# Attention with routed experts: block counts by rounding, and a written order of all steps

## The chip, the cores and the metric

The kernel runs on one core of one Trainium2 chip. The metric is the device time of one execution in microseconds (us), taken as the median of several runs. A core has five engines with queues of their own: TensorE (PE in the profile; PEld is its loading of weights), VectorE (DVE), ScalarE (ACT), GpSimd (POOL) and SyncE (SP), which here only issues DMAs. Each engine takes its instructions strictly in the order in which the program put them, so an instruction that waits holds up all that stand behind it on its engine.

## The reference

Random-feature attention over 8 batches, 8 heads, 576 positions and a head dimension of 64 with 128 features is followed by a mixture of experts with one expert for each token (4608 tokens of 512 numbers, 8 experts with a hidden width of 1024):

```python
def phi(x):
    h = einsum('bhsd,md->bhsm', x, omega) - sum(x * x, axis=-1, keepdims=True) / 2
    return exp(h - max(h, axis=-1, keepdims=True)) / sqrt(m)
q_p, k_p = phi(q * scale), phi(k * scale)
kv, z = einsum('bhsm,bhsd->bhmd', k_p, v), sum(k_p, axis=2)
x = einsum('bhsm,bhmd->bhsd', q_p, kv) / (einsum('bhsm,bhm->bhs', q_p, z)[..., None] + 1e-6)
...
logits = x @ w_gate
e_idx = argmax(logits, axis=1)
for e in range(E):
    mask = e_idx == e
    ye = maximum(x[mask] @ w1[e], 0) @ w2[e]
    out[mask] = gate_w[mask, None] * eom[mask, e, None] * ye
```

`gate_w` is the softmax probability of the chosen expert, `eom` the sigmoid of `x @ w_output_gate`. Between the two parts x is laid out as one row for each token.

## The kernel before

**Units.** The attention is cut into 32 units: four super-chunks of two batches (1152 tokens, nine tiles of 128) times eight heads. Unit `u` loads its keys and queries twice, transposed (`ld.t`) and natural (`ld.n`), and its values (`ld.v`). Its steps: `pp` projects in three groups (L631); `mx` takes the smallest number of each row (L650); `sqa` and `sqr` sum the squares (L556 on ScalarE for unit 0 and from unit 8 on, `fold` at L576 to L580 on GpSimd for units 1 to 7; then L561 or L590 on VectorE); `nb` makes the bias of the exponential (L657, L661); `ex` is the exponential (L667); `eh` and `el` cut it into two f16 halves (L691 on ScalarE, L693 on GpSimd); `eT` turns the queries' features by a DMA (units 8 on; `tq`, `th` and `tl` do it on TensorE before). `kv` multiplies keys by values (L766), `kvh`/`kvs` halve the product (L784, L786), `kt`, `ke`, `kg`, `gh`, `gl` bring in the gates (L804 to L827), `pn` multiplies by the queries (L840), `xf` divides (L849 to L853), `xh` and `xl` cut the result into halves (L870, L874), `rows` stores them to DRAM.

**Routing.** After the eighth unit of each super-chunk j, VectorE works out what goes to which expert, in chains of small instructions on tables of 8 to 192 columns: `route`, `counts` (on TensorE: the running number of earlier tokens of the same expert, L1017 to L1027), `ranks`, `places`, `gates`, `weigh`, then for group g = j `table`, `assign`, `lists`, `controls`, `gi`, `advance`. A block has 128 tokens of one expert. Whole blocks are counted by turning a float into an integer, shifting it right by 7 and turning it back (L1049 to L1053, L1074 to L1079).

**Items.** A block is an item `n`, at most 49 of them, of which 38 run for these inputs (there are 38 gathers at L1572). `gx` gathers its rows on GpSimd (L1572), `xt` turns them by a DMA, `hA` and `hB` are the two halves of the first product (L1609), `relu` and `rest` cut the hidden values into halves on ScalarE and VectorE (L1616, L1620), `out` is the second product (L1640, or L1632 for an item with at most 64 tokens), `os` scales (L1693), `put` scatters the rows to the output on GpSimd (L1682). In the last group `hB` also holds the first half of the second product, so that only `out.n.1` follows. Where the expert changes, `bring` loads the new weights and `sw` cuts them into f16 halves; from item 25 on this goes by quarters, `swh` on ScalarE (L474) and `swl` on VectorE (L478). Whether it happens is known on the chip only: each engine loads a flag into a register (`flag`) and jumps. Items 38 and on stand behind such a jump.

**The order.** Every step is registered with `plan.add` (or `plan.chain`, one step for each instruction of a chain), with its engine, an estimated cost, a rank and what it follows. `Plan.order` (L287) then plays the program through with those costs: it takes, again and again, the step of lowest rank among those that could start soonest, ranks being moved by the table `SHIFT` (L76). `emit` (L1720) writes the instructions in the order that comes out, and that fixes each engine's queue. The PSUM banks are given out in the same way: the one that came free first.

Below, a step is named as in `kvs.25` (step, unit) or `out.25.1` (step, item, half); `mx`, `ex`, `eh`, `el` count keys and queries (`el.63` is the queries of unit 31) in turn, and `nb` counts units; a trailing `s` as in `table.0.2s` is a step inside a chain.

Of the kernel before, what the change touches and what calls it, by code (L numbers as in the profile page):

```python
# [72 lines left out]
UNIT_STEPS = tuple("hi lo sqa sqr pp tq th tl eT kv kvh kvs kt ke kg gh gl pn xf xh xl lga vh vl".split())  # L73
SLOT_STEPS = tuple("gx xt hA hB relu rest out os put sw swh swl bring".split())

SHIFT = {  # L76
    "advance": (-91.89, -199.63, -64.41,),
    "again": (0.0, 0.0, 0.0, 31.03,),
    "assign": (94.42, 64.4, 10.74, -5.41,),
    "bounded": (17.08, 13.53, 102.01, -16.15,),  # L80
    "bring": (-149.34, -144.98, -146.36, 16.69,),
    "const": (-12.6,),
    "controls": (-6.33, -38.05, -43.46, 95.17,),
    "counts": (-129.68, -194.11, 15.85, -107.74,),
    "eT": (0.4, 138.19, 61.6, 50.0,),
    "eh.k": (-0.7, -0.7, -4.51, 129.09,),
    "eh.q": (-0.7, -150.18, -1.08, 50.41,),
    "el.k": (1.4, 1.4, -54.14, -117.65,),
    "el.q": (1.4, -16.84, 91.6, -1.02,),
    "ex.k": (-31.78, 38.41, -6.63, -47.76,),  # L90
    "ex.q": (-20.34, 43.13, -3.54, 100.75,),
    "flag": (1.44,),
    "gate_exps": (61.95, 151.43, -245.24, -105.03,),
    "gates": (198.78, 115.38, 308.76, 145.18,),
    "gh": (-114.02, 44.58, -83.1, -4.31,),
    "gi": (-45.91, -100.94, 157.46, 201.04,),
    "gid": (0.0, 0.0, 0.0, -258.93,),
    "gl": (-220.24, -52.52, 14.91, 135.3,),
    "gx": (-233.8, 53.3, 108.33, -107.89,),
    "hA": (202.43, 203.85, 165.91, 123.74,),  # L100
    "hB": (102.44, 10.62, 75.55, -131.59,),
    "hi": (-1.4, -9.33, -61.41, 41.14,),
    "ke": (-119.21, 53.41, -58.62, -21.2,),
    "kg": (10.71, -73.95, -95.07, 122.55,),
    "kt": (-83.5, 22.25, -22.42, -41.82,),
    "kv": (-21.36, -31.1, -28.61, -26.36,),
    "kvh": (-48.28, -277.94, -84.66, -68.07,),
    "kvs": (11.17, -54.16, -170.98, -1.28,),
    "ld.n": (-18.72, -45.88, 99.01, 42.74,),
    "ld.t": (-18.62, -9.42, -106.08, 12.44,),  # L110
    "ld.v": (-15.0, -168.92, 67.12, 3.22,),
    "lga": (-126.07, -176.33, -150.87, 10.21,),
    "limits": (0.0, 0.0, 0.0, -74.63,),
    "lists": (234.87, 96.12, 15.36, 88.59,),
    "lo": (0.3, -72.57, 152.95, 119.66,),
    "mx": (7.85, 3.5, 87.64, 51.53,),
    "nb": (-8.03, 66.86, 56.7,),
    "os": (25.69, -10.82, 137.36, 17.68,),
    "out": (144.39, 45.75, 2.51, -0.53,),
    "pid": (149.39, 102.18, 69.01, -48.7,),  # L120
    "places": (42.24, -56.95, -75.3, -34.34,),
    "pn": (-121.01, -17.46, -25.99, 68.57,),
    "pp": (-23.92, 181.9, -27.84, 189.02,),
    "put": (-10.97, -0.64, -26.58, 80.94,),
    "ranks": (84.94, -45.33, -111.8, 137.76,),
    "relu": (109.14, -112.65, 102.51, 25.06,),
    "rest": (90.98, 95.59, 184.25, -102.14,),
    "route": (56.37, 197.97, -111.62, 78.22,),
    "rows": (50.29, 102.01, 155.46, -159.35,),
    "scales": (66.65, -76.99, -69.39, 128.92,),  # L130
    "sqa": (-182.65, 164.78, 45.98, 169.51,),
    "sqr": (-47.23, 74.7, 121.64, -85.06,),
    "sw": (109.96, 40.72, -32.62,),
# [96 lines left out]

# [1552 lines left out]
```

## Time and profile before

| | us |
|---|---|
| median of 3 runs | 660.61 (658.88 to 662.42) |
| the profiled execution | 663.06 |
| its span, first to last instruction | 661.2 |
| TensorE busy in the span | 598.8 |
| VectorE busy | 430.0 |
| ScalarE busy | 411.8 |
| GpSimd busy | 368.7 |
| mean granted clock of TensorE | 0.964 |

A line of the profile's groups gives source line, engine, operation, output and inputs, shape, count, busy time in us, mean ns of one, and the idle time of the engine just before, with what ended it. A line of the timeline begins with the start and the length in us; in brackets stands the idle time before it and what ended that. A "q" behind an engine (ACTq, DVEq) is that engine's sequencer: a register or a jump. The table of stretches has busy us and the number of instructions of PE, PEld, DVE, ACT and POOL, then the granted clock of TensorE, the DMA engines' share and GB/s.

### The profile page before, as it was taken

What the parts mean: (1) busy time and instruction counts of PE and PEld (TensorE: products, weight loads), DVE (VectorE), ACT (ScalarE), POOL (GpSimd) and SP (SyncE); (2) the same over time, 40 slices, a digit from 0 to 9 for tenths busy, and PEclk for the clock granted to TensorE, in tenths of its full rate; (3) what the DMA queues carried; (4) which work ended last, traced back from release to release, by engine and by line L of the source; (5) the groups of instructions that cost most, each with busy time, mean ns of one, the idle gap of its engine ahead of it and who ended that gap; (6) DMA issues with size and microseconds to landing.
All of it is one profiled execution on the core that took longest, in us unless ns stands there. A gap on an engine that the chain in (4) does not pass through costs nothing. (4 is left out here: it accounts for less than half of the span.)

```text
span 661.2 us, 21673 instructions
## 1 busy us (share of the span) xinstructions
PE 598.8 (91%) x8444; PEld 463.2 (70%) x8444; DVE 430.0 (65%) x1140; ACT 411.8 (62%) x968; POOL 368.7 (56%) x263
## 2 busy tenths in 40 slices
...
GB/s 301 364 264 205 243 221 222 233 258 233 236 294 257 217 225 210 221 194 295 292 183 211 121 181 156 129 111 260 169 145 205 216 70 177 229 84 70 239 142 8
DMA packets 147041, 133.75 MB, mean 202 GB/s; under 512 B 104398, under 2 KB 127568, under 8 KB 145616
## 3 DMA queue, kind: packets, MB, share of 16 engines
...
## 5 line engine op out<-in xcount | busy, mean ns | idle before, releaser
L1609 PE MATMUL ph<-xt,w1h 128*128 128x128 f16 (+1 forms) x2432 | 203.3, 217 | 2.2 <-PE po L1632 1.0
L1609 PE MATMUL ph<-xt,w1l 128*128 128x128 f16 (+1 forms) x1216 | 199.6, 217 | 0.0
L667 ACT ACTIVATE ef<-pp,nb 128x128 f32<-128x128 f32 x576 | 162.7, 389 | 54.8 <-DVE nb L661 46.6
L1609 PEld LDWEIGHTS <-w1h 128*128 128x128 f16 x2432 | 180.4, 98 | 9.8 <-issue 3.1
L1620 DVE SCALAR_TENSOR_TENSOR hl<-ph,hh 128x512 f16<-128x512 f32 (+1 forms) x76 | 50.6, 666 | 117.9 <-ACTq L1538 73.2
L693 POOL TENSOR_TENSOR es<-ef,es 128x1152 f16<-128x1152 f32 x44 | 105.1, 2399 | 34.1 <-ACT es L691 28.9
L650 DVE TENSOR_REDUCE pp<-pp 128x3 f32<-128x384 f32 x192 | 103.7, 558 | 22.2 <-PE pp L631 16.8
L1609 PEld LDWEIGHTS <-w1l 128*128 128x128 f16 x1216 | 118.0, 98 | 0.0
L1572 POOL DMA_INDIRECT gx<-rows,gi x38 | 39.2, 1033 | 134.8 <-ACTq L1538 67.0
L1640 PE MATMUL po<-w2l,hh 128*128 128x512 f16 x280 | 106.9, 382 | 3.3 <-DVE w2l L478 3.3
L1640 PE MATMUL po<-w2h,hl 128*128 128x512 f16 x280 | 106.8, 382 | 1.8 <-DVEq L1533 1.8
L1640 PE MATMUL po<-w2h,hh 128*128 128x512 f16 x280 | 107.0, 382 | 0.8 <-DVE hl L1620 0.8
L1640 PEld LDWEIGHTS <-hh 128*128 128x128 f16 x560 | 52.3, 99 | 57.0 <-issue 2.6
L1616 ACT ACTIVATE hh<-ph 128x512 f16<-128x512 f32 (+1 forms) x76 | 44.3, 584 | 69.8 <-PE ph L1609 63.8
L546 POOL TENSOR_TENSOR xlo<-xt,xhi 128x1152 f16<-128x1152 f32 x24 | 58.3, 2429 | 19.4 <-ACT xhi L539 19.2
L1693 ACT ACTIVATE os<-po,gx 128x512 f32<-128x512 f32 (+1 forms) x38 | 25.5, 672 | 69.1 <-PE po L1640 61.9
L840 PE MATMUL pn<-kvs,et 128*128 128x81 f16 (+1 forms) x960 | 47.9, 207 | 10.8 <-DVE kvs L827 4.3
L1640 PEld LDWEIGHTS <-hl 128*128 128x128 f16 x280 | 27.5, 98 | 39.6 <-issue 4.6
L840 PEld LDWEIGHTS <-et 128*128 128x128 f16 (+1 forms) x960 | 40.6, 103 | 19.1 <-issue 9.0
L691 ACT CAST es<-ef 128x1152 f16<-128x1152 f32 x44 | 50.8, 1173 | 2.7 <-DMA et<-es 2.7
L874 POOL TENSOR_TENSOR xs<-xf,xs 128x576 f16<-128x576 f32 x32 | 42.6, 1332 | 7.1 <-DVE xs L870 3.9
L631 PE MATMUL pp<-omh,xhi 64*128 64x128 f16 x432 | 42.8, 222 | 2.4 <-ACT ef L667 0.7
...
## 6 DMA issues: line engine op xcount, KB each, us to landing
...
```

Of the source, the lines that this page charges most:

```text
L546: lambda t0=t0, t1=t1: nc.gpsimd.tensor_tensor(out=xl(u)[:, t0:t1], in0=xt32(u)[:, t0:t1], in1=xh(u)[:, t0:t1], op=ALU.subtract),
L631: nc.tensor.matmul(banks["pp", 2 * u + i, g][:, c, :], x[r, t], w[r, :], start=(a == 0), stop=(a == len(ops) - 1))
L650: nc.vector.tensor_reduce(out=spare(g, 0)[:, i], in_=banks["pp", 2 * u + i, g][:, 0:3, :], op=ALU.min, axis=AX.X)
L667: nc.scalar.activation(ef(2 * u + i)[:, c, :], banks["pp", 2 * u + i, g][:, c % 3, :], AF.Exp, bias=nb(u)[:, i, c : c + 1], scale=-SK)
L691: nc.scalar.copy(es(slot_es(n))[:, 0], ef(n))
L693: nc.gpsimd.tensor_tensor(out=es(slot_es(n))[:, 1], in0=ef(n), in1=es(slot_es(n))[:, 0], op=ALU.subtract)
L840: nc.tensor.matmul(pn[lo:hi, c - c0, :], a[:, c, lo:hi], w[:, b, :], start=(i == 0), stop=(i == len(ops) - 1))
L874: nc.gpsimd.tensor_tensor(out=x[:, :, P + o : P + o + D], in0=xf(u)[:, :, 0:D], in1=x[:, :, o : o + D], op=ALU.subtract)
L1609: nc.tensor.matmul(ph[:, f4, 0:w_], w[qd][:, kk, fo : fo + P], xt(n)[:, x, 0:w_], start=(a == 0), stop=(a == 3 * KC - 1))
L1616: nc.scalar.activation(hh(n)[:, sl, 0:w_], banks["ph", n, g][:, :, 0:w_], AF.Relu)
L1620: nc.vector.scalar_tensor_tensor(out=hl(n)[:, sl, 0:w_], in0=banks["ph", n, g][:, :, 0:w_], scalar=0.0, in1=hh(n)[:, sl, 0:w_], op0=ALU.ma ...
L1640: nc.tensor.matmul(po, x(n)[:, f, :], w[f // 2][:, f % 2, :], start=(f == 0 and a == 0), stop=(f == FC - 1 and a == 2))
```

## The change

Three things are changed in the text of the kernel.

**Block counts by rounding.** All positions are kept as numbers of tokens, shifted by 63.5, and not as numbers of blocks. Adding and taking away 1.5 x 2^23 x 128, where a float has steps of 128, leaves the nearest multiple of 128: one instruction in place of three. The running count `cnt` goes into `counts` by two f32 matmuls with the identity, in place of an addition in `ranks`. `last` becomes the first column of `exs`, which saves a copy; the copy `cp` moves from `lists` to `places`.

```diff
+MIDDLE = (P - 1) / 2
+ROUND = 1.5 * 2.0**23 * P
...
 def counts(j):
-    nc.tensor.matmul(pos[:, 0:NC, :], tri, one, start=True, stop=False)
+    nc.tensor.matmul(pos[:, 0:NC, :], ident, cnt.unsqueeze(1).broadcast_to([P, NC, NE]), start=True, stop=False)
+    nc.tensor.matmul(pos[:, 0:NC, :], tri, one, start=False, stop=False)
...
+    nc.tensor.matmul(pos[:, NC, :], ident, cnt, start=True, stop=False)
     for c in range(NC):
-        nc.tensor.matmul(pos[:, NC, :], ones, one[:, c, :], start=(c == 0), stop=(c == NC - 1))
+        nc.tensor.matmul(pos[:, NC, :], ones, one[:, c, :], start=False, stop=(c == NC - 1))
 def ranks(j):
-    nc.vector.tensor_tensor(out=pk, in0=pos[:, 0:NC, :], in1=cnt..., op=ALU.add)
-    nc.vector.tensor_tensor(out=cnt, in0=cnt, in1=pos[:, NC, :], op=ALU.add)
-    nc.vector.tensor_tensor(out=pk, in0=pk, in1=rt[j]["one"], op=ALU.mult)
+    nc.vector.tensor_tensor(out=pk, in0=pos[:, 0:NC, :], in1=rt[j]["one"], op=ALU.mult)
+    nc.vector.tensor_copy(cnt, pos[:, NC, :])
 def places(j):
-    nc.vector.tensor_copy(ri, rank)
-    nc.vector.tensor_scalar(ri, ri, 7, None, ALU.arith_shift_right)
-    nc.vector.tensor_copy(key, ri)
-    nc.vector.scalar_tensor_tensor(out=rank, in0=key, scalar=-float(P), in1=rank, op0=ALU.mult, op1=ALU.add)
+    if j < NSC - 1:
+        nc.vector.tensor_copy(cp, cft[:, C_BOTH : C_BOTH + 2 * nt].rearrange("p (c a) -> p c a", a=2))
+    nc.vector.tensor_scalar(key, rank, ROUND, ROUND, ALU.add, ALU.subtract)
+    nc.vector.tensor_tensor(out=rank, in0=rank, in1=key, op=ALU.subtract)
 def table(g):
-    nc.vector.tensor_scalar(av_i, cnt, float(P - 1) if g == NG - 1 else 0.0, None, ALU.add)
-    nc.vector.tensor_scalar(av_i, av_i, 7, None, ALU.arith_shift_right)
-    nc.vector.tensor_tensor(out=av, in0=av_i, in1=done[:, 0, :], op=ALU.subtract)
-    nc.vector.tensor_tensor(out=t["av"], in0=av_i, in1=done[:, 0, :], op=ALU.subtract)
+    if g == NG - 1:
+        nc.vector.scalar_tensor_tensor(out=av, in0=cnt, scalar=float(P - 1), in1=done, op0=ALU.add, op1=ALU.subtract)
+        nc.vector.tensor_scalar(t["av"], av, ROUND, None, ALU.add)
+        nc.vector.tensor_scalar(av, av, ROUND, None, ALU.add)
+    else:
+        for x in (av, t["av"]):
+            nc.vector.scalar_tensor_tensor(out=x, in0=cnt, scalar=ROUND, in1=done, op0=ALU.add, op1=ALU.subtract)
 def assign(g):
-    nc.vector.tensor_copy(ex[:, 1, 0:1], last)
```

`first_state` loses one copy; `limits`, `advance` and `controls` keep their number of instructions, with other constants. The number of steps goes from 3231 to 3208.

**GpSimd.** No line of the diff touches `squares` (L567 to L594), in which GpSimd folds the squares of units 1 to 7.

**A written order.** `SHIFT`, the ranks and the costs are gone. `Plan.order` reads a list of 3208 numbers, which are the steps in the order of their registration, and a string of digits, the bank that each step takes. It asserts that no step stands ahead of what it follows:

```diff
     def order(self):
+        numbered = list(self.steps.values())
+        out = [numbered[int(x)] for x in ORDER.split()]
+        done, taken, free = set(), iter(BANKS.replace("\n", "")), set(range(8))
+        turner = None
+        for s in out:
+            kind = s["key"][0]
+            s["behind"] = turner if kind in ("gx", "put") else None
+            turner = s["key"] if kind == "eT" else turner
...
+            for _, name, _ in s["bank"]:
+                self.bank_of[name] = int(next(taken))
+                free.remove(self.bank_of[name])
             for name in s["frees"]:
+                free.add(self.bank_of[name])
         return out
...
+ORDER = """
+31 0 32 5 36 34 37 87 86 39 40 45 4 33 2 1 146 35 38 41 95 89 7 88 10 3 42 51 46 47 52 43 44 53 48 90 49 57 54 98 58
...
+BANKS = """
```

Turned back into names, the queues read as follows at some places (a line for before, then one for after):

```
VectorE, start     mx.0.0 mx.1.0 sqr.0 mx.0.1 nb.0.0.0s mx.0.2 nb.0.0 mx.1.1
                   mx.0.0 mx.1.0 mx.0.1 sqr.0 nb.0.0.0s nb.0.0 mx.0.2 mx.1.1
TensorE, unit 8    pp.9.2 pp.10.0 kt.8 counts.0 kv.9.0 kv.9.1 kg.8 pp.10.1 pp.10.2 pn.8.0 pn.8.5 kt.9 kg.9 pid.0
                   pp.9.2 kt.8 counts.0 pp.10.0 kv.9.0 kv.9.1 kg.8 pn.8.5 pn.8.0 pp.10.1 pp.10.2 kt.9 kg.9 pid.0
TensorE, item 4    hB.4 out.4.0 pn.14.5 kv.15.0 kv.15.1 pp.16.2 pp.17.0 out.4.1
                   hB.4 pp.16.1 pn.14.5 kv.15.0 kv.15.1 out.4.0 pp.16.2 pp.17.0 out.4.1
TensorE, item 12   hA.13 hB.13 out.12.0 out.12.1 pn.22.0 pn.22.5
                   hA.13 hB.13 pn.22.0 out.12.0 out.12.1 pn.22.5
VectorE, unit 25   lists.2 controls.2.3s kvh.25 controls.2.4s (xf.24 and advance.2, eleven steps) kvs.25
                   lists.2.0s kvh.25 rest.15.0 (two of controls.2, two of xf.24) lists.2 controls.2.3s kvs.25
VectorE, unit 25   mx.52.2 flag.16 mx.53.2 sw.16.1 nb.26.2.0s gl.25
                   mx.52.2 gl.25 flag.16 mx.53.2
VectorE, unit 30   rest.20.0 sw.21.1 rest.20.1 kvh.31 gl.30 kvs.31
                   rest.20.0 sw.21.1 gl.30 kvh.31 kvs.31 rest.20.1
GpSimd, unit 31    el.62 gx.22 put.19 el.63 lga.30
                   el.62 gx.22 el.63 lga.29 put.20 put.19
TensorE, item 25   hA.25 hB.25 out.25.1 hA.26 hB.26
                   hA.25 hB.25 hA.26 out.25.1 hB.26
ScalarE, item 25   relu.25.0 swh.26.1.0 swh.26.1.1 relu.25.1 swh.26.1.2 swh.26.1.3
                   relu.25.0 swh.26.1.1 swh.26.1.0 swh.26.1.2 relu.25.1 swh.26.1.3
VectorE, item 25   rest.25.0 swl.26.1.0 swl.26.1.1 rest.25.1 swl.26.1.2 swl.26.1.3
                   rest.25.0 swl.26.1.0 swl.26.1.1 swl.26.1.3 rest.25.1 swl.26.1.2
TensorE, item 36   hA.35 hB.35 out.35.1 hA.36 hB.36 out.36.1 hA.37 hB.37 out.37.1
                   hA.35 hB.35 hA.36 out.35.1 hB.36 out.36.1 hA.37 hB.37 out.37.1 flag.38
```

(In the rows of item 25, steps of a change of expert that does not take place are left out.)

More of the change, by code (lines that the diff above doesn't have):

```diff
@@ L72 @@
 NBUF = {}
[L73 to L133, printed above, removed]
-    "swh": (0.0, 0.0, 0.0, 64.83,),
-    "swl": (0.0, 0.0, 0.0, 37.18,),
-    "table": (-17.26, 106.56, -46.43, -184.0,),
-    "th": (-115.17,),
-    "tl": (8.41,),
-    "tq": (-19.6,),
-    "vh": (0.0, 0.0, 57.39, -65.33,),
-    "vl": (0.0, 0.0, -64.28, 185.62,),
-    "w0": (163.19,),
-    "w0h": (165.2,),
-    "w0l": (121.85,),
-    "weigh": (102.85, -159.77, -133.91, -253.47,),
-    "xf": (-38.12, -72.54, 231.75, -24.26,),
-    "xh": (-41.36, -173.75, -90.78, 73.08,),
-    "xl": (-30.84, -87.19, -154.38, -66.61,),
-    "xt": (-59.86, -203.12, -22.07, 7.46,),
-}
@@ L153, in place_of @@
-def place_of(key):
-    a, i = key[0], key[1] if len(key) > 1 else 0
-    if a == "ld":
-        return f"ld.{i}", key[2], "unit"
-    if a in ("ex", "eh", "el"):
-        return f"{a}.{'kq'[i % 2]}", i // 2, "unit"
-    if a in ("mx", "nb"):
-        return a, i // 2, "unit"
-    if a in UNIT_STEPS:
-        return a, i, "unit"
-    if a in SLOT_STEPS:
-        return a, i, "slot"
-    if a == "rows":
-        return a, i // NP, "part"
-    return a, 0 if a in ("flag", "w0", "w0h", "w0l", "const") else next((x for x in key[1:] if isinstance(x, int)), 0), "part"
@@ L171, in shift @@
-def shift(key):
-    name, i, kind = place_of(key)
-    steps = {"unit": (8, 12, 24), "slot": (8, 16, 25), "part": (1, 2, 3)}[kind]
-    at = SHIFT.get(name, (0.0,))
-    return at[min(sum(i >= x for x in steps), len(at) - 1)]
 TIE = 0.1
@@ L1208, in limits @@
         nc.vector.scalar_tensor_tensor(
[L1209 removed]
+            out=lim, in0=t["off"][:, 0, :], scalar=-1.0, in1=cnt, op0=ALU.mult, op1=ALU.add
         )
@@ L1346, in routing @@
         chain(
-            "ranks", (0.14, 0.08, 0.14, 0.14), ranks, [("counts", j)] + [("table", g) for g in old],
+            "ranks", (0.14, 0.08, 0.14), ranks, [("counts", j)] + [("table", g) for g in old],
             frees=[("pos", j)],
         )
-        chain("places", (0.07, 0.07, 0.07, 0.08, 1.27), places, [("ranks", j)])
+        chain("places", (0.1, 0.07, 0.08, 1.27) if j < NSC - 1 else (0.07, 0.08, 1.27), places, [("ranks", j)])
         chain("gates", (0.14, 0.14, 0.14), gates, [("route", j)], rank=R + 0.1)
```

214 lines of the change are left out of this document (62 added, 152 removed), and 128 rows, old and new, of the table ORDER.

## The prediction

> **What bounds the kernel now.** I read the profile's page first, then the table of stretches, then the gaps of TensorE in order of time, and at each gap the queue of the engine that ended it.
>
> ```profile
> span 661.2 us, 21673 instructions
> PE 598.8 (91%) x8444; PEld 463.2 (70%) x8444; DVE 430.0 (65%) x1140; ACT 411.8 (62%) x968; POOL 368.7 (56%) x263
> 80.00:100.00 20.00, 16.75 (x219) 14.61 (x218) 16.40 (x47) 15.23 (x42) 7.96 (x5) 0.74 0.72 232
> 100.00:120.00 20.00, 12.05 (x168) 10.15 (x161) 18.74 (x79) 10.65 (x31) 12.26 (x8) 0.79 0.94 234
> 160.00:180.00 20.00, 20.00 (x322) 15.28 (x320) 12.37 (x36) 18.06 (x44) 16.98 (x11) 1.00 0.86 231
> 648.30:661.20 12.90, 0.00 (x0) 0.00 (x0) 0.00 (x0) 0.47 (x1) 0.98 (x1) 0.59 0.03 8
> ```
>
> The columns behind the stretch are busy us of PE, PEld, DVE, ACT, POOL, then the granted clock, DMA share and GB/s. TensorE is the bound: 598.8 of 661.2 us, and in 160 to 180 it has no gap. So the order can only win where TensorE stands still: 661.2 - 598.8 = 62.4 us. Of these 12.9 lie behind the last matmul (the last scatter landing) and 5.1 before the first; nothing in the change touches them. Some 44 us are left, and they are many small gaps. In 100 to 120, the first routing, TensorE works 12.05 of 20 us and VectorE 18.74: there VectorE is the bound.
>
> The gaps on which the sum rests (start, duration, instruction, then idle time before it and what ended it):
>
> ```profile
> 13.11 0.99 PE L720 MATMUL tq<-ident,ef 128*128 128x128 f32 x3 [2.50 <-ACT ef L667]
> 115.92 0.41 PE L1277 MATMUL pid<-r_itc,place 128*128 128x16 f16 x9 [1.26 <-DVE r_itc L1157]
> 201.47 0.39 PE L1640 MATMUL po<-w2h,hl 128*128 128x512 f16 x1 [1.75 <-DVEq L1533]
> 337.62 0.38 PE L1640 MATMUL po<-w2l,hh 128*128 128x512 f16 x1 [1.46 <-DVE w2l L478]
> 376.24 0.30 PE L804 MATMUL kv<-cmt,kvs 128*64 128x128 f16 x4 [0.97 <-DVE kvs L786]
> 381.98 0.84 PE L840 MATMUL pn<-kvs,et 128*128 128x81 f16 x18 [1.29 <-DVE kvs L827]
> 464.56 0.30 PE L804 MATMUL kv<-cmt,kvs 128*64 128x128 f16 x4 [1.53 <-DVE kvs L786]
> 477.23 1.41 PE L840 MATMUL pn<-kvs,et 128*128 128x81 f16 x30 [1.26 <-DMA et<-es]
> 521.66 0.42 PE L1632 MATMUL po<-w2h,hh 128*64 128x256 f16 x2 [2.70 <-ACT w2h L474]
> 637.52 0.30 PE L1632 MATMUL po<-w2h,hh 128*64 128x256 f16 x2 [0.74 <-PE po L1632]
> 638.21 0.30 PE L1632 MATMUL po<-w2h,hl 128*64 128x256 f16 x2 [0.28 <-DVE hl L1620]
> 643.26 0.30 PE L1632 MATMUL po<-w2h,hh 128*64 128x256 f16 x2 [0.56 <-ACT hh L1616]
> 645.35 0.30 PE L1632 MATMUL po<-w2h,hl 128*64 128x256 f16 x2 [1.68 <-DVE hl L1620]
> ```
>
> **The routing's arithmetic.** These groups carry the instructions that go, and the nearest to one that comes; the columns are count, busy us, mean ns, idle time ahead.
>
> ```profile
> L1033 DVE TENSOR_TENSOR rt<-pos,cnt 128x72 f32<-128x72 f32 x4 | 0.9, 234 | 0.5 <-PE pos L1027 0.5
> L1049 DVE CAST rt<-rt 128x9 int32<-128x9 f32 x4 | 0.7, 172 | 0.1
> L1051 DVE TENSOR_SCALAR rt<-rt 128x9 int32<-128x9 int32 x4 | 0.7, 174 | 0.1
> L1053 DVE CAST keys<-rt 128x9 f32<-128x9 int32 x4 | 0.7, 167 | 0.1
> L1074 DVE TENSOR_SCALAR rt<-cnt 128x8 int32<-128x8 f32 x4 | 0.7, 167 | 0.1
> L1076 DVE TENSOR_SCALAR rt<-rt 128x8 int32<-128x8 int32 x4 | 0.7, 174 | 0.1
> L1116 DVE COPY rt<-last 128x1 f32<-128x1 f32 x3 | 0.5, 158 | 0.0
> L809 PE MATMUL kv<-wgr,kvf 128*128 128x32 f32 x64 | 11.6, 266 | 1.7 <-ACT kvf L815 1.6
> ...
> 103.50 0.21 PE L1017 MATMUL pos<-r_one,cmt 128*128 128x72 f16 x1 [0.71 <-DVE r_one L980]
> 222.36 0.19 PE L1017 MATMUL pos<-r_one,cmt 128*128 128x72 f16 x1 [0.88 <-DVE r_one L980]
> ```
>
> In groups 0 to 2 six instructions go: the addition of `cnt` (0.234), two of the three that made `key` (L1049, L1051 and L1053 become one, which I price at the 174 ns of L1051: 0.172 + 0.167), the two of L1074 and L1076 (0.341) and the copy of `last` (0.158): 1.07 us. In group 3 five go, 0.90, since one rounding comes back. That is 3 x 1.07 + 0.90 = 4.1 of 430 us of VectorE. The copy of L1146 moves from `lists` to `places`, ahead of the wait that it stood in. It is on the path only where VectorE is the bound, in the first routing. `counts` gains two f32 matmuls, 72 and 8 columns wide, which the trace does not show. Between nothing (they run while the group waits for the one-hot) and 2 x 0.27 a group (L809). I take nothing in groups 0 and 1, whose first matmul waited 0.71 and 0.88 us for the one-hot, and 0.3 each in groups 2 and 3, which show no such wait: **+0.6 us**.
>
> **GpSimd's folding** has no line in the diff: lines 567 to 594 do it already. I count nothing.
>
> **The order, place by place.** I decoded the numbers into steps and compared each engine's queue. TensorE keeps its sequence but for single swaps; VectorE, ScalarE, GpSimd and SyncE are shuffled within some ten places. What follows is for the places whose queues I could follow.
>
> - Start: `nb.0.0` now follows `sqr.0` at once.
>
> ```profile
> 9.39 1.35 DVE L561 TENSOR_REDUCE sqs<-sqt 128x18 f32<-128x1152 f32 x1 [1.36 <-ACT sqt L556]
> 11.66 0.15 DVE L661 SCALAR_TENSOR_TENSOR nb<-pp,sqs 128x6 f32<-128x6 f32 x1
> ```
>
>  Before, `mx.0.1` and `mx.0.2` ran between the end of `sqr.0` (10.74) and `nb.0.0` (11.66); now the first runs in the 1.36 us of idle before `sqr.0`, the second after. The bias is ready at about 10.74 + 0.15 instead of 11.81: **-0.85**, and the 2.50 us gap shrinks by it.
> - First routing: between `lga.7` and the end of `lists.0` VectorE loses the 1.07 us, and swaps leave about 0.5 more behind it (`mx.18.2` goes ahead, `nb.9.1` comes in). The gap at 115.92 is 1.26, with others before it: **-1.6**; at least 0, at most the 20.00 - 12.05 us of that stretch.
> - Item 4 (gap at 201.47): `out.4.0` waited for `rest.4.0`. Now `pn.14.5`, `kv.15.0` and `kv.15.1`, which came next behind it, stand ahead. Their work is four ninths of the 1.41 at 477.23 and the 1.04 of such a `kv`: **-1.7**.
>
> ```profile
> 456.50 1.04 PE L766 MATMUL kv<-vs,es 128*128 128x65 f16 x28 [0.68 <-POOL es L693]
> L1620 DVE SCALAR_TENSOR_TENSOR hl<-ph,hh 128x512 f16<-128x512 f32 (+1 forms) x76 | 50.6, 666 | 117.9 <-ACTq L1538 73.2
> ```
>
> - Item 12 (337.62): `pn.22.0` goes ahead of `out.12.0`, 0.84 us of work by its like at 381.98: **-0.84**.
> - Third routing: `kvs.25` stood behind seven steps of dividing and advancing (gap 0.97); now it comes straight after `lists.2`. `gl.25` stood behind `mx.53.2`, which itself waited for TensorE (gap 1.29); now it is ahead: **-2.26** together.
> - Last units: `gl.30` and `kvs.31` go ahead of `rest.20.1` (0.67, L1620) and `gl.30` ahead of one more; `pn.30.5` goes ahead of `kt.31`: -0.9 of 1.53. On GpSimd `el.63` goes ahead of `put.19`, so the transposition of unit 31 starts about 1 us sooner: -1.0 of 1.26. Together **-1.9**.
> - Item 25, half full, before the change of expert at 26:
>
> ```profile
> 517.63 2.36 DVE L478 SCALAR_TENSOR_TENSOR w1l<-ef,w1h 128x1024 f16<-128x1024 f32 x2 [0.58 <-ACT w1h L474]
> 525.43 0.29 PE L1609 MATMUL ph<-xt,w1h 128*128 128x128 f16 x2 [1.00 <-PE po L1632]
> 528.87 0.28 PE L1609 MATMUL ph<-xt,w1h 128*128 128x128 f16 x2 [0.59 <-PE ph L1609]
> 517.40:519.00 1.60, 1.50 (x24) 1.23 (x24) 1.00 1.05 420
> 521.60:524.50 2.90, 2.77 (x24) 2.05 (x24) 0.51 0.49 194
> ```
>
>  Before: `hB.25`, `out.25.1`, `hA.26`, `hB.26`. Now `hA.26` stands ahead of `out.25.1`, and ScalarE cuts a third quarter before `relu.25.1`. `hA.26` needs the first two quarters of w1l, about 520.8 on VectorE; then 2.9 us of it, then 1.5 of `out.25.1`: `hB.26` begins near 525.3 instead of 528.87, **-3.6**. In that lie 1.27 us of clock: the same 24 matmuls took 1.50 at full and 2.77 at half clock. The new price is `rest.25.1`, behind one more `swl` (1.2 us); it is late only if `hA.26` ends before about 522.4.
> - Last items, 36 and 37, with a change of expert between: `hA.36` goes ahead of `out.35.1`, so the cutting for 37 starts 2.7 us sooner in TensorE's work. Of the four waits (0.74 + 0.28 + 0.56 + 1.68 = 3.26) I take **-2.1**; the rest is VectorE's own cutting. The flags for 38 move to the end of the queues, behind item 37's work, and lie beside the last scatter, which the 12.9 us already hold.
>
> Sum: 0.85 + 1.6 + 1.7 + 0.84 + 2.26 + 1.9 + 3.6 + 2.1 = 14.85 won, 0.6 lost.
>
> **New waits.** Some two thousand other steps move too, and the trace cannot show their waits. One sort I could count from the list: a PSUM bank taken again within two places of the step that frees it happens 16 times, before never. The nearest row is a wait for ScalarE to empty a bank:
>
> ```profile
> 85.03 0.98 PE L840 MATMUL pn<-kvs,et 128*128 128x81 f16 x12 [1.81 <-ACT ef L667]
> 340.94 0.38 PE L1640 MATMUL po<-w2l,hh 128*128 128x512 f16 x1 [1.86 <-DVE w2l L478]
> ```
>
> Bounds: -15 (gaps that I did not read shrink as those that I read did) to 16 x 1.81 = +29. I take two such waits, **+3.6**, near the lower end, because all eight places that I read move the right way.
>
> Total -14.85 + 0.6 + 3.6 = -10.65. The profiled execution took 663.06 us (span 661.2 and 1.86 around it) and would be 652.4; the median of 660.61 becomes **650**.
>
> A rule to weigh: the Trainium skill, "TensorE: Matmul & The Clock Gate", "What's actually happening", lets the clock fall after an idle window of about 3.4 us. The stretch 521.60 to 524.50 shows 0.51 behind a gap of 2.70, and no gap in the middle of the trace reaches 3.4. By the rule the half clock would not come from the gap and would stay: the sum would be 1.3 less. The row decides.
>
> **Rivals.**
> 1. The gaps only move: each filled wait comes back at the next step, because DMA (0.94 busy in 100 to 120) or ScalarE sets the pace. Left are the 1.07 us of the first routing and the 2.1 at the end, where nothing follows, less 0.6: 660.6 - 2.6 = **658**. For it: in 80 to 100 VectorE and ScalarE are as full as TensorE (16.40 and 15.23 against 16.75 us), so a swap there only changes which one waits. Against: in 160 to 180 TensorE runs without a gap.
> 2. More is filled than I read: the 14.25 net without a new wait, and 8 of the other 26 us of gaps (44 less the 18 quoted above): 660.6 - 22 = **638**. For it: all that I read shrank; against: some of them, as the 1.81 at 85.03, hang on loads whose place in the queue is the old one.
> 3. Slower: banks. If TensorE waits 1.81 us at twelve of the sixteen retaken banks, +21.7, and the 14.25 net are won: **668**. It decides from eight such waits on (14.25 / 1.81 = 7.9). For it: the list fixes banks, where the planner took the bank that it held free first. Against: nearness in the list is not nearness in time.
> 4. The change doesn't do what it says: the list is the old order but for the routing. The decoded queues speak against it; it would give 660.6 - 1.07 + 0.6 = **660**.
>
> **How the numbers follow.** Forecast 0.57, rival 1 0.17, rival 2 0.16, rival 3 0.07, rival 4 0.03. A measurement of this kernel can tell about 0.5% from no change, 3.3 us. Faster by more: 0.57 + 0.16 + a fifth of rival 1 = 0.77; within: the rest of rivals 1 and 4, 0.16; slower 0.07. The range reaches from rival 2 to rival 1 with the shown runs' spread (658.88 to 662.42) on it: **638 to 660**. Outside lie rival 3, half of rival 2 and a part of 1 and 4: some 0.18.
>
> **What would show it.** Right: the stretch 100 to 120 with over 13.5 us of TensorE; the 2.70 us gap between the two halves of item 25's second product under 2.0, with `hA.26` between them and a clock of 1.00 in 520 to 540; the waits of the last two items under 1.5 together; VectorE's total near 426 (430.0 - 4.1). Wrong: TensorE's idle time within 3 us of 62.4, or a number of new waits on `ef L667` or `et L727` over 1.5 us in front of `pp`, `pn`, `kv`.

## The result and the profile after

The changed kernel takes 683.85 us (median of 4 runs, 681.5 to 686.86) against 659.93 for the kernel before (4 runs, 658.88 to 662.42): a ratio of 1.0359, 95% interval 1.0298 to 1.0421. The forecast of 650 was wrong in sign, and 638 to 660 did not hold it. Ratios, here and below, leave out a run that is more than 1.5% above the fastest of its kernel.

First the page of the changed kernel, then its table of stretches (columns as in the prediction).

```profile
span 684.2 us, 21664 instructions
PE 608.4 (89%) x8460; PEld 472.0 (69%) x8460; DVE 428.4 (63%) x1116; ACT 413.6 (60%) x968; POOL 361.9 (53%) x263
```

```profile
100.00:120.00 20.00, 14.81 (x215) 13.10 (x215) 18.76 (x91) 13.94 (x42) 9.94 (x7) 0.76 0.97 221
200.00:220.00 20.00, 13.49 (x170) 11.11 (x170) 15.39 (x20) 9.22 (x20) 14.60 (x10) 0.83 0.77 178
340.00:360.00 20.00, 16.11 (x211) 10.74 (x209) 10.30 (x28) 13.09 (x34) 13.57 (x9) 0.91 1.05 234
460.00:480.00 20.00, 16.38 (x242) 14.61 (x242) 7.60 (x12) 12.14 (x27) 12.52 (x8) 0.83 0.77 210
520.00:540.00 20.00, 13.48 (x191) 9.69 (x189) 7.92 (x11) 6.95 (x9) 3.80 (x4) 0.93 0.81 225
```

Two of these stretches in the kernel before:

```profile
200.00:220.00 20.00, 18.52 (x286) 13.81 (x287) 14.44 (x39) 16.33 (x42) 15.41 (x11) 1.00 0.84 246
460.00:480.00 20.00, 17.22 (x216) 12.36 (x215) 13.94 (x27) 9.20 (x14) 9.67 (x7) 0.91 0.76 193
```

The last matmul ends at 666.65 (before: 648.3). So the 23.0 us between the two spans split three ways. Behind the last matmul lie 17.55 us instead of 12.9: 4.65. TensorE's idle time ahead of it went from 661.2 - 598.8 - 12.9 = 49.5 to 684.2 - 608.4 - 17.55 = 58.25: 8.75. And its busy time grew by 9.6, of which the 16 records of the new f32 matmuls are 3.2. The mean granted clock fell from 0.964 to 0.947, and it is 0.83 in 200 to 220 (1.00 before) and in 460 to 480 (0.91 before), so some of the rest are slower matmuls behind gaps. How much is open: e5 below is as long as the changed kernel, with 607.7 us of TensorE busy, at a mean clock of 0.964.

The first routing went as forecast (14.81 us of TensorE in 100 to 120, over the 13.5 named). The loss is elsewhere. The view of GpSimd's waits (line, whom it waited for, us in total, times, longest) shows what is new, the changed kernel first, then the one before:

```profile
POOL out L1625 <- DMA out<-os,oi: 16.5, 5, 4.0
POOL out L1625 <- ACTq L1476: 13.3, 2, 6.7
POOL out L1625 <- DMA out<-os,r_oi: 6.8, 3, 3.1
```

```profile
POOL out L1682 <- DMA out<-os,r_oi: 0.9, 1, 0.9
```

A scatter (`put`) waits until the scatter ahead of it has landed. The wait belongs to the program: in the instructions built from either kernel, each `put` waits for the semaphore that the `put` ahead of it in the queue raises when it lands (both write `out`), though no line of kernel.py names it. No run here took that wait out. Before, while units run, one stands some seven GpSimd steps behind the other, and only one wait of 0.9 us is put down to it. The new list pairs them: `put.2` and `put.3` follow each other at once, so do `put.14` and `put.15`, `put.17` and `put.18`; and in six places the later one stands ahead, as `put.11` of `put.10`, `put.20` of `put.19`, `put.36` of `put.35`. The second of a pair stands still for up to 4 us and all of GpSimd with it. The 6.7 us put down to a jump of ScalarE (ACTq) stand ahead of `put.3`; its rows were scaled by 190.1 (from 189.41, 0.68 us), the transposition that the program ties it to had landed by 191.8 (issued at 183.99, 7.8 us to landing), and `put.2` landed at 199.9 (192.18 and 7.7). So that wait is for the landing of `put.2` too.

The worst pair, in the timeline of GpSimd, VectorE, ScalarE and TensorE of the changed kernel (start, length, idle time before):

```profile
192.18 1.81 POOL L1625 DMA_INDIRECT out<-os,oi  x1 [0.16 <-issue]
200.68 1.00 POOL L1625 DMA_INDIRECT out<-os,oi  x1 [6.68 <-ACTq L1476]
201.71 2.38 POOL L637 TENSOR_TENSOR es<-ef,es 128x1152 f16<-128x1152 f32 x1
204.05 1.41 POOL L658 TENSOR_TENSOR vs<-rawv,vs 128x650 f16<-128x650 f32 x1
205.42 2.37 POOL L490 TENSOR_TENSOR xlo<-xt,xhi 128x1152 f16<-128x1152 f32 x1
207.75 1.41 POOL L658 TENSOR_TENSOR vs<-rawv,vs 128x650 f16<-128x650 f32 x1
201.27 8.25 DVE L814 CAST xs<-xf 128x576 f16<-128x576 f32 x1
211.15 0.89 ACT L611 ACTIVATE ef<-pp,nb 128x128 f32<-128x128 f32 x3 [7.23 <-DVE nb L605]
212.25 0.41 PE L753 MATMUL kv<-wgr,kvf 128*128 128x32 f32 x2 [3.95 <-ACT kvf L759]
```

GpSimd idles 6.68 us, then runs four operations without a break. VectorE's cast of unit 14 (`xh.14`), 0.48 us in its group's undisturbed rows, begins just ahead of them and ends when the fourth ends: 8.25 us. Behind it the bias, the exponential and TensorE's `kg` are late. `os.3` began 7.75 us earlier than before (189.41 against 197.16), `os.4` 5.02 later (214.43 against 209.41).

Three more pairs, each with a later row that waited (GpSimd, then ScalarE or TensorE); that the pair is what each of them waited for is a reading here, which e9 tests:

```profile
335.10 1.55 POOL L1625 DMA_INDIRECT out<-os,oi  x1 [3.38 <-DMA out<-os,oi]
345.48 0.38 PE L710 MATMUL kv<-vs,es 128*128 128x65 f16 x7 [3.53 <-ACTq L1476]
410.76 1.00 POOL L1625 DMA_INDIRECT out<-os,oi  x1 [3.87 <-DMA out<-os,oi]
422.15 0.38 PE L710 MATMUL kv<-vs,es 128*128 128x65 f16 x7 [1.49 <-DVE kvs L771]
456.31 0.98 POOL L1625 DMA_INDIRECT out<-os,oi  x1 [3.98 <-DMA out<-os,oi]
460.30 4.67 POOL L637 TENSOR_TENSOR es<-ef,es 128x1152 f16<-128x1152 f32 x2
462.69 1.66 ACT L611 ACTIVATE ef<-pp,nb 128x128 f32<-128x128 f32 x6 [7.87 <-POOL es L637]
463.62 0.43 PE L710 MATMUL kv<-vs,es 128*128 128x65 f16 x5 [4.09 <-ACT ef L611]
```

The last pair stands at the end, where nothing follows that could hide it:

```profile
661.01 2.05 POOL L1625 DMA_INDIRECT out<-os,r_oi  x1 [18.76 <-ACT os L1636]
665.98 0.97 POOL L1625 DMA_INDIRECT out<-os,r_oi  x1 [2.92 <-DMA out<-os,r_oi]
671.26 0.47 ACT L1636 ACTIVATE os<-po,gx 128x256 f32<-128x256 f32 x1 [6.41 <-PEq L1676]
```

`put.36` goes first, at 661.01, after 18.76 us for its rows, while `put.35` stands behind it; `put.35` must then wait for its landing, and `os.37`, which takes the buffer that `put.35` reads, begins 4.6 us after the last matmul.

### The profile page after: what moved, and what is told of

Read it like the earlier page. It is cut to its first block, busy times and chain, and to the rows that moved or that the text cites. A ratio compares the mean times of both kernels' runs of the same rounds, so it can differ in the third digit from the quotient of the medians.

```text
span 684.2 us, 21664 instructions
## 1 busy us (share of the span) xinstructions
PE 608.4 (89%) x8460; PEld 472.0 (69%) x8460; DVE 428.4 (63%) x1116; ACT 413.6 (60%) x968; POOL 361.9 (53%) x263
## 5 line engine op out<-in xcount | busy, mean ns | idle before, releaser
L1552 PE MATMUL ph<-xt,w1h 128*128 128x128 f16 (+1 forms) x2432 | 210.9, 221 | 8.1 <-issue 5.5
L1552 PE MATMUL ph<-xt,w1l 128*128 128x128 f16 (+1 forms) x1216 | 206.4, 220 | 1.0 <-DVE w1l L422 1.0
L611 ACT ACTIVATE ef<-pp,nb 128x128 f32<-128x128 f32 x576 | 165.9, 386 | 66.1 <-DVE nb L605 33.9
L1552 PEld LDWEIGHTS <-w1h 128*128 128x128 f16 x2432 | 185.4, 100 | 15.6 <-issue 8.3
L594 DVE TENSOR_REDUCE pp<-pp 128x3 f32<-128x384 f32 x192 | 106.0, 560 | 35.1 <-PE pp L575 27.8
L1552 PEld LDWEIGHTS <-w1l 128*128 128x128 f16 x1216 | 120.5, 100 | 1.1 <-DVE w1l L422 1.1
L1636 ACT ACTIVATE os<-po,gx 128x512 f32<-128x512 f32 (+1 forms) x38 | 25.7, 676 | 65.4 <-PE po L1583 52.6
L818 POOL TENSOR_TENSOR xs<-xf,xs 128x576 f16<-128x576 f32 x32 | 41.5, 1300 | 25.6 <-DVE xs L814 22.9
L784 PEld LDWEIGHTS <-et 128*128 128x128 f16 (+1 forms) x960 | 41.0, 105 | 14.9 <-issue 4.1
L1625 POOL DMA_INDIRECT out<-os,oi x25 | 26.6, 1065 | 40.9 <-DMA out<-os,oi 16.5
```

Source lines behind the costliest of these rows:

```text
L594: nc.vector.tensor_reduce(out=spare(g, 0)[:, i], in_=banks["pp", 2 * u + i, g][:, 0:3, :], op=ALU.min, axis=AX.X)
L611: nc.scalar.activation(ef(2 * u + i)[:, c, :], banks["pp", 2 * u + i, g][:, c % 3, :], AF.Exp, bias=nb(u)[:, i, c : c + 1], scale=-SK)
L784: nc.tensor.matmul(pn[lo:hi, c - c0, :], a[:, c, lo:hi], w[:, b, :], start=(i == 0), stop=(i == len(ops) - 1))
L818: nc.gpsimd.tensor_tensor(out=x[:, :, P + o : P + o + D], in0=xf(u)[:, :, 0:D], in1=x[:, :, o : o + D], op=ALU.subtract)
L1552: nc.tensor.matmul(ph[:, f4, 0:w_], w[qd][:, kk, fo : fo + P], xt(n)[:, x, 0:w_], start=(a == 0), stop=(a == 3 * KC - 1))
```

## The experiments

Each run had runs of the kernel before beside it on its own chip; chips differ (medians of before from 661.93 to 665.62 beside the experiments), so only the ratios are compared. The other columns are from the profiled executions: the start of the row that scales an item (`os`, L1693 before, L1636 here) less that in the profile of before, in us. Runs of identical code differ by up to 4 us in them (e9 and e10 are the same up to `os.24`), so the steps from one column to the next say more than the columns.

| kernel | ratio to before (95%) | os.3 | os.4 | os.13 | os.19 | os.24 | os.26 | os.34 | os.37 |
|---|---|---|---|---|---|---|---|---|---|
| changed | 1.0359 (1.0298 to 1.0421) | -7.8 | +5.0 | +5.0 | +18.9 | +12.8 | +16.2 | +17.1 | +22.9 |
| e1 arithmetic, old order | 1.0056 (1.0015 to 1.0097) | -1.5 | -0.9 | +1.7 | +1.8 | +1.5 | +0.4 | +0.4 | +2.0 |
| e2 one cast moved | 1.022, two runs, no interval | -9.7 | -2.5 | -1.3 | +12.2 | +6.3 | +9.7 | +11.3 | +19.2 |
| e3 new until item 3 | 1.0050 (1.0024 to 1.0076) | -0.4 | +1.2 | +6.0 | +6.4 | +6.1 | +6.6 | +7.0 | +7.3 |
| e4 new from item 25 | 1.0185 (1.0128 to 1.0243) | -1.1 | -0.5 | +3.0 | +3.3 | +4.3 | +6.3 | +7.2 | +14.2 |
| e5 all scatters at old places | 1.0272 (1.0243 to 1.0302) | -3.1 | +4.8 | +9.8 | +20.4 | +16.3 | +18.3 | +20.6 | +22.4 |
| e6 last pair in order | 1.0302 (1.0268 to 1.0336) | -6.7 | +6.4 | +6.7 | +19.6 | +13.8 | +16.9 | +18.4 | +19.6 |
| e7 old order, pairs | 1.0165 (1.0137 to 1.0193) | -3.1 | +1.2 | +5.5 | +12.6 | +10.2 | +9.1 | +9.0 | +9.2 |
| e8 put.2 apart | 1.0241 (1.0204 to 1.0278) | -7.7 | +0.4 | -0.3 | +12.8 | +7.0 | +10.6 | +12.3 | +17.6 |
| e9 pairs parted | 1.0083 (1.0046 to 1.0119) | -10.2 | -1.0 | -3.7 | +2.1 | -4.7 | -1.2 | -0.6 | +1.9 |
| e10 e9, old tail | 1.0045 (1.0007 to 1.0083) | -7.8 | +2.0 | -0.8 | +4.8 | -1.0 | +1.2 | +1.0 | +2.2 |
| e11 banks by rule | 1.0342 (1.0263 to 1.0422) | -7.2 | +5.5 | +5.4 | +14.4 | +11.4 | +14.9 | +16.2 | +21.7 |
| e12 e9, hA back | 1.0119 (1.0077 to 1.0161) | -10.0 | -2.1 | -2.9 | +3.7 | -2.3 | +1.2 | +2.1 | +4.4 |
| e13 e10, put.15 later | 0.9980 (0.9948 to 1.0012) | -8.2 | -0.2 | -0.6 | +6.5 | +0.6 | -0.6 | -0.1 | +1.3 |

The edits are all in the written list (and the bank digits that go with it); they are shown as steps.

**e1, the arithmetic alone.**

```diff
-ORDER = the new list
+ORDER = the steps in the sequence of the kernel before, with its banks
```

> The new routing arithmetic with the old order: the written list holds the steps in the sequence, and with the banks, of the kernel before. If the loss of 24 us comes from the order alone, this is 657 to 660 us (1.07 us less of VectorE in the first routing, up to 0.6 more on TensorE). If the arithmetic itself costs time (its scalar_tensor_tensor of 8 columns shows 0.17 us in the first routing, but 1.27 and 0.55 in the second, 1.20 and 1.82 in the third), it is 662 to 665.

1.0056: on the scale of 659.93 us that is 663.6, in the range named for the case that the arithmetic itself costs time. So the arithmetic costs some 0.6% (0.15 to 0.97), and the other 3% of the loss are the order's. In the profile VectorE falls to 424.0 us, and from the gates of unit 6 to those of unit 8 (`gl`, across the first routing) 2.9 us are gained, but by item 13 that is gone and more. The arithmetic wins where it was forecast, and at the end that is a small loss.

**e2, one cast moved.**

```diff
-VectorE  rest.4.1 kvh.15 kvs.15 xh.14 mx.32.2
+VectorE  xh.14 rest.4.1 kvh.15 kvs.15 mx.32.2
```

> The changed kernel with one step moved: VectorE casts the result of unit 14 (xh.14) ahead of rest.4.1, kvh.15 and kvs.15 and not behind them, so that it runs before GpSimd's four two-input operations in a row (201.7 to 209.2). Theory of the shared path between VectorE and GpSimd: the cast takes 0.5 us where it took 8.25, and the time falls by 6 to 12 us, to 672 to 678. Rival, the loss is spread over many new waits (banks, order) and this stall only hides them: within 2 us of 683.85.

The cast takes its normal time, in VectorE's timeline of this kernel:

```profile
198.31 0.49 DVE L814 CAST xs<-xf 128x576 f16<-128x576 f32 x1
```

From `os.3` to `os.4` the loss shrinks from 12.8 to 7.2 us. The total is not settled. Of the four runs (676.49, 682.32, 687.24, 687.9; before 664.57) two count, and their 1.022 lies in the range of the theory (672 to 678 us, 1.018 to 1.027) without an interval; the other two lie in that of the rival. e8 says more on whether the stall of the cast is the root.

**e3 and e4, the list in pieces.**

```diff
 e3
-ORDER = the new list
+ORDER = the first 1050 steps of the new list, the rest in the old sequence
 e4
-ORDER = the new list
+ORDER = the first 2451 steps in the old sequence, the rest as in the new list
```

> New arithmetic; the first 1050 of 3208 steps (up to unit 13 and item 3) in the new order, the rest in the old. The changed kernel was 7.75 us ahead at item 3. If that lead is real and the loss arises behind it, 650 to 654 us. If the lead is only work that was put off (other steps of the same stretch are late), it is given back by item 5 and the time is 657 to 661.

1.0050, some 663 us on the scale of 659.93, nearer to the 657 to 661 of the second case than to the 650 to 654 of the first: the lead of 7.75 us at item 3 was work put off. With the old order from there on, only 0.4 us of it are there at `os.3`, and by `os.13` it is 4.3 us behind e1.

> New arithmetic; the first 2451 steps in the old order, the last 757 (the change of expert at item 26 and all behind it) in the new. The changed kernel lost 3.4 us from item 24 to 26 and 6 over items 34 to 37 against before. If these losses belong to the order of the tail, 664 to 670 us. If they follow from the delays ahead of it (where the loads and the instruction stream stand when it begins), 657 to 661.

The tail's own order costs about 10 us (from +4.3 at `os.24` to +14.2 at `os.37`; 0.5 in e1). The ratio of 1.0185 is some 672 us, above the 664 to 670 expected. Of the 10 us, 7 lie between `os.34` and `os.37`, where the last pair stands (e6). Its other parts that run did not tell apart; e10 bears on them.

**e5 and e6, scatters moved back.**

```diff
 e5: every put.n among the GpSimd steps that it stood among before
 e6
-GpSimd  gx.37 put.34 put.36 put.35 (flags) put.37
+GpSimd  gx.37 put.34 put.35 put.36 (flags) put.37
```

> The changed kernel with only the scatters moved: each put stands in GpSimd's queue where it stood in the kernel before (among the same gathers and casts), so that no two follow each other but put.21 and put.22. Theory: a scatter waits for the landing of the one ahead of it, and GpSimd stands still for that time (in the changed kernel 23 us on eight waits put down to the scatter's own DMA, and 6.7 us ahead of put.3 and put.22); what stands behind it then runs in a row and locks out VectorE. Then 14 to 24 us go: 660 to 670. Rival, VectorE's cast and the tail's cutting order are causes of their own: 4 to 8 us go: 676 to 680.

1.0272, some 6 us where 14 to 24 were expected: a miss. All but one of the waits for a landing are gone (3.6 us of 23.3), but other waits stand in their place, as the view of GpSimd's waits of e5 shows (`put.34` and `put.35`, too, still follow each other):

```profile
POOL out L1625 <- ACT xhi L483: 8.4, 1, 8.4
POOL out L1625 <- ACT ef L611: 5.2, 1, 5.2
POOL out L1625 <- DVE xs L814: 5.1, 1, 5.1
POOL out L1625 <- DMA out<-os,r_oi: 3.6, 1, 3.6
```

My reading, which no run tests by itself: in the new order the old neighbours of a scatter run at another time against the items, so the scatter came up before what it needs was there, and GpSimd stood still for that. Parting the pairs is thus not enough by itself; the place that a scatter gets instead decides.

> The changed kernel with put.35 ahead of put.36 again, nothing else. In the changed kernel the last product ended at 666.65 and os.37, which takes os.35's buffer, began at 671.26. By the theory of the scatters os.37 begins within 0.3 us of the last product's end: 4.6 us less, 679. By the rival (os.37 waits for TensorE's jump at the end, 4.8 us, whose queue the flags for item 38 now stand in) it still begins 4 to 5 us late: within 1 us of 683.85.

ScalarE's timeline of e6 shows `os.37` released by the last product; from `os.34` to `os.37` this kernel loses 1.2 us where the changed one lost 5.7. The rival (the jump at the end) is out. The ratio of 1.0302, 3.8 us under 1.0359, agrees, but the intervals overlap.

```profile
668.02 0.47 ACT L1636 ACTIVATE os<-po,gx 128x256 f32<-128x256 f32 x1 [1.91 <-PE po L1575]
```

**e7, the reverse.**

```diff
 nine times, as here
-GpSimd  gx.5 put.2 xl.13 lga.13 vl.16 lo.17.0 el.30 gx.6 put.3
+GpSimd  gx.5 xl.13 lga.13 vl.16 lo.17.0 el.30 gx.6 put.2 put.3
```

> The reverse: new arithmetic with the old order (median 666.5 when it ran alone), but nine scatters paired as in the new list: put.2 next to put.3, 14 to 15, 17 to 18, and put.5, 10, 19, 22, 30 and 35 directly behind the scatter after them. Theory of the scatters: 10 to 25 us more than the same order without the pairs, 676 to 690. Rival (the pairs lie beside other work and only the new order makes them late): 664 to 669.

1.0165 against 1.0056 of the same order without pairs: about 7 us, under the 10 that I gave as the least. In GpSimd's timeline of e7 two of the waits, ahead of `put.3` and of `put.5`:

```profile
203.18 1.01 POOL L1625 DMA_INDIRECT out<-os,oi  x1 [4.40 <-DMA out<-os,oi]
251.02 1.00 POOL L1625 DMA_INDIRECT out<-os,oi  x1 [5.58 <-DMA out<-os,oi]
```

Behind the first one the lag grew by 4.3 us from `os.3` to `os.4` (0.7 in e1), and behind the second by 8.2 from `os.6` to `os.7`. Part of it was given back by `os.13`; from there to `os.19`, with two more pairs, it grew by 7.1 (0.1 in e1), and behind that no more. So the pairs cost time in the old order too, but less than in the new one, though GpSimd waits longer for landings here (23.4 + 5.3 us against 16.5 + 6.8).

**e8, one pair parted.**

```diff
-GpSimd  lo.17.0 (...) xl.13 el.30 put.2 put.3 el.31 vl.16 lo.18.0 vl.17
+GpSimd  lo.17.0 put.2 xl.13 el.30 put.3 el.31 vl.16 lo.18.0 vl.17
```

> The changed kernel with put.2 alone moved to its old place, so that put.3 no longer follows it at once. Theory: GpSimd does not stand still ahead of put.3 (6.68 us), its next four operations no longer meet VectorE's cast of unit 14, and the cast takes under 2 us with nothing moved on VectorE; from item 3 to item 4 the changed kernel's loss of 12.8 us shrinks to under 4. In all 6 to 12 us less, 672 to 678. Rival (the cast is locked out whatever GpSimd did before): still over 6 us for the cast.

```profile
183.77 1.01 POOL L1625 DMA_INDIRECT out<-os,oi  x1 [0.16 <-issue]
193.44 1.37 POOL L1625 DMA_INDIRECT out<-os,oi  x1 [0.60 <-ACT w2h L418]
```

In GpSimd's timeline of e8 `put.3` waits 0.60 us instead of 6.68, the cast of unit 14 takes 0.48 us again, and of TensorE's three gaps there (1.30, 3.95, 1.27) only the first is left, at 1.38. From `os.3` to `os.4` it still loses 8.1 us (expected: under 4), but 2.1 of them are back at `os.5`. In all 1.0241 against 1.0359: 8 us by one scatter, with VectorE's queue untouched. The cast was the second link of the chain here, the pair the first.

**e9, the pairs parted where GpSimd had room.**

```diff
 GpSimd
+put.2  behind lo.17.0      +put.5  ahead of lo.20.0   +put.10 ahead of lo.25.0
+put.14 ahead of lga.24     +put.15 ahead of xl.25     +put.17 ahead of xl.26
+put.19 behind gx.22        +put.22 ahead of gx.25     +put.35 ahead of put.36
```

> The changed kernel with nine scatters moved earlier and nothing else: put.2, 5, 10, 14, 15, 17, 19 and 22 each to a place in GpSimd's queue where its scaled rows (os) were ready and GpSimd stood idle or ran on, put.35 ahead of put.36. Five of the pairs stand ahead of the five largest gaps of TensorE in the changed kernel: 1.30 + 3.95 + 1.27 behind put.3, 3.53 behind put.10, 0.88 + 1.49 + 0.76 behind put.15, 4.09 behind put.18, and 4.6 us from the last product to os.37 behind put.35: 21.9 us. Theory: 16 to 22 us go, a ratio to before of 1.002 to 1.012. Rival (as when all scatters were put where the old order had them, ratio 1.027: the waits only move to other steps of the new order): 1.02 to 1.03.

1.0083, in the range of the theory: 18 of the 24 us are gone, with nine of 3208 steps moved. GpSimd's waits of e9 for a landing:

```profile
POOL out L1625 <- DMA out<-os,r_oi: 3.4, 2, 2.7
POOL out L1625 <- DMA out<-os,oi: 0.8, 1, 0.8
```

GpSimd does not wait less in front of its scatters for that. All rows of that view with `out` add up to 90.4 us in e9, as in the changed kernel (89.6; 53.1 before, 70.8 in e5). The scatters now stand earlier and wait there, by the rows for their own data or for a transposition; that GpSimd's next work was not needed yet at these places is a reading. What e9 shows is that these nine places cost 18 us; that the wait for a landing costs by itself, wherever it stands, it does not show.

**e10 and e12, what is left in the tail.**

```diff
 e10: e9, and
-ORDER from step 2451 on = the new list
+ORDER from step 2451 on = the old sequence
 e12: e9, and on TensorE
-hB.25 hA.26 out.25.1 hB.26      hB.35 hA.36 out.35.1 hB.36
+hB.25 out.25.1 hA.26 hB.26      hB.35 out.35.1 hA.36 hB.36
```

> The same with the last 757 steps (from the change of expert at item 26 on) in the old order. If the new tail loses by more than its scatters (hA.26 and hA.36 ahead of out.25.1 and out.35.1, quarters cut in another sequence), this is 3 to 6 us faster than with the pairs parted alone, a ratio of 0.995 to 1.005. If the tail's loss was the scatters', no difference over 2 us.

1.0045: 2.5 us better by the medians, at the edge of what can be told; the intervals overlap. The 3 to 6 us expected of the tail are not shown. With its scatters parted the new tail costs little more than the old one, which suggests that most of e4's loss was the scatters'.

> The kernel with the pairs parted (ratio 1.0083), and on TensorE hA.26 and hA.36 put back behind out.25.1 and out.35.1, nothing else. In that kernel items 24 to 26 took 3.6 us longer than before (on TensorE 3.78 us without a recorded wait after the third matmul of hA.26) and items 34 to 37 2.5 us longer. Theory (the prediction's step for item 25 has the wrong sign: hA.26 ahead only waits for its weights and holds out.25.1 behind it): items 24 to 26 lose under 2 us and the ratio falls to 1.000 to 1.006. Rival (hA.26 ahead gains as predicted, and the loss comes from the sequence of the quarters): 3 us slower there, a ratio of 1.010 to 1.016.

From `os.24` to `os.26` it loses 3.5 us, as e9 did (3.55). The first row is TensorE's in e9, the second the one that takes its place in e12:

```profile
521.24 0.37 PE L1552 MATMUL ph<-xt,w1h 128*128 128x128 f16 x2 [3.78 <-issue]
```

```profile
522.19 0.43 PE L1575 MATMUL po<-w2l,hh 128*64 128x256 f16 x2 [2.38 <-DVEq L1481]
```

With `hA.26` ahead TensorE does three of its matmuls and then stands for 3.78 us with no wait that the profile shows; with `hA.26` behind, `out.25.1` stands for 2.38 us, which the profile puts down to VectorE's sequencer. In these items neither theory is borne out: the sequence of the two products makes no difference that shows. The total, 1.0119, lies in the rival's range, but its interval overlaps with that of e9, and the loss is not where the rival put it. Whether the rest of the tail's loss is the sequence of the quarters was not tried by itself.

**e11, the banks.**

```diff
-BANKS = the written digits
+BANKS = the bank freed longest ago
```

> The changed kernel with the PSUM banks given out by a rule (the one freed longest ago) in place of the list's digits: 472 of the steps that take a bank get another, and no bank is taken within two places of being freed unless no other is free. Rival 3 of the prediction (waits on retaken banks): at least 5 us less than 683.85. Theory of the scatters: the same within 3 us, a ratio of 1.03 to 1.04.

1.0342, in the range of the theory of the scatters: 1.1 us under the changed kernel, which the intervals (some 5 us each way) do not tell from nothing. Of the 472 digits 409 differ (472 is their number, not that of the steps that change). Banks taken again within two places fell from 16 to 4, and nothing like the 21.7 us of rival 3 went with them.

**e13, one more scatter.**

```diff
 e10, and
-GpSimd  el.53 put.15 xl.25 gx.18 vl.28 el.54
+GpSimd  el.53 xl.25 gx.18 vl.28 el.54 put.15
```

> The kernel with the pairs parted and the old tail (ratio 1.0045), and put.15 moved behind el.54. Where it stood, GpSimd waited 7.14 us at it (the list ties a scatter to the transposition ahead of it), and el.54, the exponentials and kv.27 behind it came late (2.75 us of TensorE). If a scatter's place holds up what stands behind it here too, os.17 comes 2 to 4 us earlier and the ratio falls to 0.998 to 1.002, about the kernel before. If that time only moves, no difference over 1 us.

0.9980, 0.65% under e10 and level with the kernel before; but it ran on another chip than e10, and the intervals meet (to 1.0012 here, from 1.0007 there). In e10 GpSimd stood 7.14 us at `put.15`, and TensorE behind it; in e13 that gap of TensorE is not there. The rest of the forecast failed: `os.17` came no earlier (+5.6 against +4.9), and GpSimd stands 5.91 us at the next step, `xl.25`, instead. So the gap went, and whether the total gained by it is not shown.

```profile
395.72 1.02 POOL L1625 DMA_INDIRECT out<-os,oi  x1 [7.14 <-ACT es L635]
403.92 1.81 PE L710 MATMUL kv<-vs,es 128*128 128x65 f16 x30 [2.75 <-ACT ef L611]
```

## Why the prediction was wrong

- **New waits (+3.6), the step that failed.** "One sort I could count from the list: a PSUM bank taken again". The sort that mattered was another: a transfer that must land before the next of its kind may go. GpSimd's rows in the prediction's comparison show it (`put.20 put.19` behind `lga.29`), and I read that row as a gain, "`el.63` goes ahead of `put.19`". That one scatter can wait for another's landing was in the waits of before (the row of 0.9 us above), which I did not read for GpSimd. I compared the queues for the sequence of their steps and not for the distance between steps of one kind. Measured: 18 us by e9, where 3.6 were taken. Of the signs that I had named for "wrong", TensorE's idle time within 3 us of 62.4 did not come (75.8); of the waits over 1.5 us on `ef` one came, 4.09 in front of `kv`, behind a pair.
- **The gains (14.85), which failed too.** The forecast lies 34 us under the measured time, and the pairs are only 18 of them. With the pairs parted (e9) the ratio is 1.0083, where 650 us would be 0.984: some 16 us are still missing, as much as all the gains together. The new arithmetic in the old order (e1) is at 1.0056, so the new order without its pairs gains nothing that these runs can tell. Single gaps closed as read (below), but their closing did not reach the end of the kernel.
- **The bounds of the new waits held, the value in them did not.** +29 was given as the upper end; the range of 638 to 660 cut it off by a chance of 0.07 for rival 3. Rival 3 had the sign (668), but by luck: its mechanism, the banks, shows no effect (e11). The argument against it, "nearness in the list is not nearness in time", holds for banks and failed for scatters, which are near in time as well.
- **Rival 1, the gaps only move, is nearest to what remains** when the scatters are out of the way. It forecast 658 for a kernel at 660.6, a ratio of 0.996; e13, with the new arithmetic, the new middle and the old tail, is at 0.9980 (0.9948 to 1.0012), e9 with the whole new list at 1.0083 (1.0046 to 1.0119). Why each filled wait came back was not tested.
- **First routing (-1.6):** right, and under-sized: e1 gains 2.9 us there by the arithmetic alone, the changed kernel 5.1, and the sign for it came (14.81 us in 100 to 120). But the gain is not in the total.
- **Counts (+0.6):** each f32 matmul shows as two records, on the mean of 0.26 and 0.29 us, 3.2 us of TensorE over four groups. I had counted one record each.
- **VectorE near 426:** 428.4, and 424.0 in e1. The new instructions cost the 0.17 us that I took for them only where GpSimd is quiet; in the third routing the two that make `av` take 1.20 and 1.82 us.
- **Start (-0.85):** the times quoted give 0.92 (11.81 less 10.89). The gap of 2.50 shrank to 0.53, but that was lost at once to a new gap of 2.30 us at 11.15, behind a load (`xt<-kqt`) that moved back in its queue.
- **Items 4 and 12, third routing, last units:** the quoted gaps went, but in the changed kernel a larger one follows each of items 4 (3.95), 12 (3.53) and the last units (4.09), all behind pairs. In e9 two of the four gaps quoted at 338, 341, 465 and 477 are gone and 0.49 and 0.21 us are left of the others (two new ones are there, 1.64 and 2.60 us), and e9 is 4.7 us ahead of before at `os.24`, e10 1.0. There the reading of single queues was right, and worth a few us at most.
- **Item 25 (-3.6), no gain:** items 24 to 26 take 3.4 us longer in the changed kernel, 3.55 in e9. That `hA.26` stands ahead is not what costs, since e12 puts it back and loses 3.5 there as well. "`hA.26` needs the first two quarters, then 2.9 us of it" left out that it would run at half clock (45 of its matmuls took 4.95 us in e9, at 0.50) and stand still for 3.78 us after the first three. The clock of 1.00 in 520 to 540, a sign for "right", was 0.93.
- **Last items (-2.1):** the waits grew from 3.26 to 4.80 (1.08 + 1.30 + 0.61 + 0.97 + 0.84), and the swapped scatters added 4.6. That the flags would "lie beside the last scatter" looked at the flags and not at the scatters themselves.
